# Taking a linear-attention numerator by pairs of token tiles, with the order of a hand-scheduled loop rewritten around it

## The chip, the cores and the metric

The kernel runs on one core of a Trainium2 chip. The metric is the device time of one execution in microseconds (us). Five engines work side by side, each through its own list of instructions in order: TensorE (PE) multiplies, VectorE (DVE), ScalarE (ACT) and GpSimd (POOL) do the elementwise work, SyncE (SP) issues DMAs. An instruction starts when its engine has reached it and the semaphores it waits for have come.

## The reference, cut to what matters

All tensors are fp32; x has 2048 tokens of width 512.

```
h  = x + A(layernorm(x))            # linear attention, 32 heads of 16
h2 = h + B(layernorm(h))            # token-mixing MLP, 2048 -> 1792 -> 2048
A: q, k, v = x @ wqkv, by heads
   phi(t) = [softmax(t @ w_phi), softmax(-t @ w_phi)]      # 32 features a head
   kv  = phi(k)^T v ;  z = sum over tokens of phi(k)
   o   = (phi(q) kv) / (phi(q) z + 1e-6)                    # numerator / denominator
   out = o @ wo
B: u = gelu(h^T w1 + b1) ;  out = (u w2 + b2)^T
```

## The kernel before, in words

The 2048 tokens are 16 tiles of 128 (`NT`). Matmuls that need precision split each operand into a rounded high part and a low rest, and take three products (`mm3`, L60: high·high, high·low, low·high); `split` (L55) makes the parts, the high one on ACT, the low one by a subtraction on another engine.

A first stage (to about 141 us) forms keys, values and the first q tiles, and sums kv and z. Then comes the loop at L630, `for it in range(NT + 3)`, on which the change works. For PE, DVE, ACT and POOL its order is the order in which the code issues (`manual_schedule`, L419); only SP, and everything after the loop, is ordered by the planner. In iteration `it` several token tiles are under way at different steps:

- POOL multiplies the exponentials of q tile it+1 by their weights (`s_pq`, L460) and forms `ez` for tile it+3 (`s_ez`, L442), from which DVE takes the denominator (`s_den`, L451 to L457: a long reduce, then five short steps) and so the weights `w`.
- DVE takes the logits of a later q tile from PSUM (`q_logits`: L151, L152, L145), POOL forms their negative half (`negate`, L159 and L160), ACT the exponentials (`q_exp`, L171), DVE their sums (`q_sums`, L216). `q_mm` projects the next q tile on PE, until all 16 are done in iteration 4.
- `s_tr(it)` (L521): PE transposes the eight 128x128 blocks of the weighted tile into the PSUM tile `tn` (one buffer), and ACT copies them to `pht` in two halves (L527).
- `s_num` (L536): sixteen small fp32 matmuls, 64 rows by 32 columns each, that stream `pht` of one tile (128 columns) against kv into `tn` again; ACT rounds the result to `oh` (L547), DVE takes the rest to `ol` (L552).
- `s_wo` (L554): twelve 128x512 matmuls of `oh` and `ol` with wo into `po` (one PSUM buffer). `s_h` (L564) adds x on DVE, which frees `po`, and sends h out. `s_moments` (ACT, L574 to L576), `s_rstd` (POOL, L579 and L580) and `s_hn` (ACT L584 and L57, POOL L58) normalise h into `hs`, in two parts.
- `fill(p)` (L616): six 128x512 matmuls of `hs` of one token tile with w1, for the pair p of MLP column blocks, accumulated over all 16 tiles into `pu`. The loop takes pairs 0 and 1, one tile behind the other; the other five pairs, and what the loop has not filled, follow after it. `fill_load` (L611) loads two tiles' worth of w1, ACT rounds it (`whi`, L604), and `flush` (L593) has DVE subtract (`wlo`, L596) at a place that the loop chooses.

On PE an iteration runs numerator of tile it-1, wo of tile it-2, transposes of tile it, a q tile, and fills from iteration 4 on (`LAG`, L28). On DVE `s_h` stands fourth in the list, the flush some places behind it. After the loop PE finishes the seven pairs, takes gelu, and multiplies with w2 (L764, from about 383 us).

Of the kernel before, what the change touches and what calls it, by code (L numbers as in the profile page):

```python
# [9 lines left out]
F32 = mybir.dt.float32  # L10
F32R = mybir.dt.float32r
# [13 lines left out]
Q_AT = (4, 6, 8, 9, 11, 13)  # L25
V_NOT = (0, 1, 11)
SUMS = 8
LAG = 4  # L28
WARM = 9
EPS = 1e-5  # L30

# [2 lines left out]
def block_kernel(ctx: ExitStack, tc: tile.TileContext, x, xT, wT, phic, wo, w1, b1, w2, b2,  # L34
# [25 lines left out]
    def mm3(o, ah, al, bh, bl, first, last):  # L60

        nc.tensor.matmul(o, ah, bh, start=first, stop=False)  # L62
        nc.tensor.matmul(o, ah, bl, start=False, stop=False)  # L63
        nc.tensor.matmul(o, al, bh, start=False, stop=last)  # L64
# [90 lines left out]
    def negate():  # L155

        if MN:
            ev, mx, mn = MN.pop(0)
            nc.gpsimd.tensor_sub(mn, mn, mx)  # L159
            nc.gpsimd.tensor_sub(ev[:, :, 1], mn.unsqueeze(3).to_broadcast([P, NPR, 2, DH]), ev[:, :, 0])  # L160

    def turns(*lists):

        return [ops[i] for i in range(max(map(len, lists))) for ops in lists if i < len(ops)]

    def run(*lists):
        for op in turns(*lists):
            op()
# [197 lines left out]
    def q_logits(lag):  # L366
        n = q["logits"]
        if n < min(NT, q["mm"] - lag + NT * (q["mm"] == NT)):
            EQ[n] = big.tile([P, NG, P], F32, name="eq", tag="big")
            q["logits"] += 1  # L370
            return logit_ops(PS[n], EQ[n], n >= len(Q_AT))
        return []
# [7 lines left out]
    def q_sums(lag):  # L380
        n = q["sum"]
        if n < min(NT, q["exp"] - lag + NT * (q["exp"] == NT)):
            q["sum"] += 1
            return q_sum(n)
        return []
# [54 lines left out]
    def s_ez(t):  # L440
        EZ[t] = az.tile([P, NG, P], F32, name="ez")
        nc.gpsimd.tensor_mul(EZ[t], EQ[t], zB)  # L442

    def s_den(t):


        tz = az.tile([P, NPR, 2, 2], F32, name="tz")
        den = az.tile([P, NPR, 2], F32, name="den")
        W[t] = az.tile([P, NPR, 2, 2], F32, name="w", bufs=3)
        other = SQ[t]  # L450
        return [lambda: nc.vector.reduce_sum(tz.rearrange("p g c h -> p (g c h)"), heads(EZ[t]), axis=AX.X),  # L451
                lambda: nc.vector.scalar_tensor_tensor(tz[:, :, 0], other[:, :, 1], 1e-6, tz[:, :, 0],
                                                       op0=ALU.mult, op1=ALU.add),
                lambda: nc.vector.tensor_mul(tz, other, tz),
                lambda: nc.vector.reduce_sum(den, tz.rearrange("p g c h -> p g h c"), axis=AX.X),
                lambda: nc.vector.reciprocal(den, den),
                lambda: nc.vector.tensor_mul(W[t], other, den.unsqueeze(2).to_broadcast([P, NPR, 2, 2]))]  # L457

    def s_pq(t):
        nc.gpsimd.tensor_mul(heads(EQ[t]), heads(EQ[t]), W[t].rearrange("p g c h -> p (g c h)").unsqueeze(2).to_broadcast([P, 2 * H, DH]))  # L460

    def lead(it, mm):

        if 0 <= it + 3 < NT:
            s_ez(it + 3)
        negate()
        for _ in range(mm):
            q_mm()
        q_exp(0)
# [49 lines left out]
    HN, HT, PHT, OS, PO, VE = {}, {}, {}, {}, {}, {}  # L519

    def s_tr(t):  # L521
        PHT[t] = ak.tile([P, NG, P], F32, name="pht")
        ptr = ps_t.tile([P, 2, 4, P], F32, name="tn")
        for g in range(NG):
            nc.tensor.transpose(ptr[:, g // 4, g % 4, :], EQ[t][:, g, :], ident)  # L525
        for half in range(2):
            nc.scalar.activation(PHT[t][:, half * 4:half * 4 + 4, :], ptr[:, half], AF.Copy)  # L527

    def s_kv():

        pt = ps_o.tile([P, 2, P], F32, name="po")
        for b in range(2):
            nc.tensor.transpose(pt[:, b, :], kvS[:, 2 * b:2 * b + 2, :].rearrange("p n f -> p (n f)"), ident)
        nc.scalar.activation(kvB, pt, AF.Copy)

    def s_num(t):  # L536

        pn = ps_t.tile([P, 2, 4, P], F32, name="tn")[:, :, 0:2]
        for b in range(2):
            for c in range(4):  # L540
                for r in range(2):
                    rows, cols = slice(64 * r, 64 * r + 64), slice(32 * c, 32 * c + 32)
                    nc.tensor.matmul(pn[cols, r, b, :], kvB[rows, b, cols], PHT[t][rows, 4 * b + c, :],  # L543
                                     start=True, stop=True, skip_group_check=True)
        oh = ak.tile([P, 2, 2, P], F32R, name="oh")
        ol = ak.tile([P, 2, 2, P], F32R, name="ol")
        nc.scalar.activation(oh, pn, AF.Copy)  # L547
        OS[t] = oh, ol, pn

    def s_ol(t):  # L550
        oh, ol, pn = OS[t]
        return [lambda: nc.vector.tensor_sub(ol, pn, oh)]  # L552

    def s_wo(t):  # L554
        oh, ol, _ = OS.pop(t)
        PO[t] = po = ps_o.tile([P, D], F32, name="po")
        for j in range(4):
            mm3(po, oh[:, j // 2, j % 2, :], ol[:, j // 2, j % 2, :], woh[:, j, :], wol[:, j, :], j == 0, j == 3)

    def s_x(t):  # L560
        HT[t] = ak.tile([P, D], F32, name="h", bufs=4)
        nc.sync.dma_start(HT[t], x[t * P:(t + 1) * P, :])

    def s_h(t):  # L564

        h = HT[t]
        VE[t] = ak.tile([P, 4], F32, name="ve2", bufs=3)
        nc.vector.scalar_tensor_tensor(h, PO.pop(t), 1.0, h, op0=ALU.mult, op1=ALU.add, accum_out=VE[t][:, 2:3])
        nc.sync.dma_start(out[t * P:(t + 1) * P, :], h)

    def s_moments(t):

        junk = ak.tile([P, D], F32, name="hj", bufs=1)
        nc.scalar.activation(VE[t][:, 1:2], VE[t][:, 2:3], AF.Copy, scale=-1.0 / D)  # L574
        nc.scalar.activation(junk, HT[t], AF.Square, bias=VE[t][:, 1:2], accum_out=VE[t][:, 3:4])
        nc.scalar.activation(VE[t][:, 0:1], VE[t][:, 3:4], AF.Identity, scale=(1.0 + EPS) / D, bias=eps2)  # L576
# [5 lines left out]
    def s_hn(t):  # L582
        hn = ak.tile([P, D], F32, name="hn")
        nc.scalar.activation(hn, HT[t], AF.Identity, scale=r2[:, t:t + 1], bias=VE[t][:, 1:2])  # L584
        HN[t] = big.tile([P, 2, D], F32R, name="hs", tag="big")
        split(HN[t][:, 0], HN[t][:, 1], hn, nc.gpsimd)
# [6 lines left out]
    def flush():  # L593
        while LATER:
            wl_, raw, wh_ = LATER.pop(0)
            LO.append(nc.vector.tensor_sub(wl_, raw, wh_).ins)  # L596
# [14 lines left out]
    def fill_load(p):  # L611
        if FL[p] < NT:
            WI[p, FL[p]] = stream(w1v, FL[p], 2, p * 256, 256)
            FL[p] += 2

    def fill(p, pool=None):  # L616

        t = FN[p]
        FN[p] = t + 1
        if FL[p] <= t:  # L620
            fill_load(p)
            flush()
        if t == 0:
            PU[p] = [pool.tile([P, D], F32, name="pu", tag="pu") for _ in range(2)]
        a, b = WI[p, t - t % 2]
        for c in range(2):
            mm3(PU[p][c], a[:, t % 2, c * P:(c + 1) * P], b[:, t % 2, c * P:(c + 1) * P],
                HN[t][:, 0], HN[t][:, 1], t == 0, t == NT - 1)

    for it in range(NT + 3):  # L630
        if 0 <= it < NT:
            s_x(it)
        if 0 <= it - 1 < NT:
            s_num(it - 1)
        if 0 <= it - 3 < NT:
            s_moments(it - 3)
        if 0 <= it - 2 < NT:
            s_wo(it - 2)
        if it == 1:
            run(q_logits(0))  # L640
            q_mm()
        if 0 <= it < NT:
            s_tr(it)
        if it == 0:
            s_kv()
        if 0 <= it + 1 < NT:
            s_pq(it + 1)
        if 0 <= it - 3 < NT:
            s_rstd(it - 3)
        lead(it, 1)  # L650
        den = s_den(it + 2) if it + 2 < NT else []
        ql = q_logits(1)
        ops = turns((s_ol(it - 1) if 0 <= it - 1 < NT else []) + ql + (q_sums(0) if it > 0 else []), den)

        at = 7 if ql else 3
        ops[at:at] = [flush]
        ops[3:3] = [lambda: s_h(it - 2)] if 0 <= it - 2 < NT else []
        run(ops)
        if it > 0:
            negate()  # L660
        if 0 <= it - 3 < NT:
            s_hn(it - 3)
        if FN[0] <= it - LAG:
            fill(0, ps_f)
        for _ in range(2):
            if q["logits"] == NT and FN[1] <= it - LAG:
                fill(1, ps_q)
        for p in range(2):
            if it >= LAG - 2 and FL[p] <= FN[p] + 1:
                fill_load(p)  # L670
    flush()
    ms.close()
# [197 lines left out]
```

## Time and profile before

| what | value |
|---|---|
| median of three runs | 530.43 us (530.4 to 531.09) |
| the profiled execution | 530.48 us |
| its span in the trace | 528.7 us, so 1.8 us lie around it |
| PE busy | 521.3 us, 99% of the span |
| DVE, ACT, POOL busy | 378.8, 272.2, 230.9 us |
| granted TensorE clock | 0.998 |
| the loop's PE work | about 142 to 271 us |

A row of the timeline gives start, duration, engine, source line, operation and `out<-in` with shapes. Durations of neighbours on one engine overlap, since each row includes the end of the pipeline; what an instruction costs its engine is the distance from its start to the start of the next. Each plain fp32 matmul stands in the trace as two records, so the numerator's sixteen appear as x32.

### The profile page before, as it was taken

How to read it: one execution, taken by the hardware profiler on the slowest of the kernel's cores; microseconds unless marked ns; L12 is line 12 of the kernel's file. 1: busy time of each engine (PE TensorE's matmuls, PEld its weight loads, DVE VectorE, ACT ScalarE, POOL GpSimd, SP SyncE). 2: the span in 40 equal slices, each digit the busy share in tenths (PEclk: the TensorE clock that was granted, in tenths of full speed). 3: DMA queues.
4: the chain of work that ended last, by engine and by line, in shares of the span. 5: the costliest groups of instructions: out<-in, count | busy, mean ns of one | idle time of the engine just before them, and what ended most of it. 6: DMA issues, size and time to landing. Idle time of an engine off the chain costs nothing.

```text
span 528.7 us, 9887 instructions
## 1 busy us (share of the span) xinstructions
PE 521.3 (99%) x3872; PEld 450.0 (85%) x3872; DVE 378.8 (72%) x680; ACT 272.2 (51%) x460; POOL 230.9 (44%) x190
## 2 busy tenths in 40 slices
PE   8999999999999999999999999999999999999996
PEld 7888888887877777777888888888899999999996
DVE  6993999876899888773426424835668878987784
ACT  6998833525237776676657323526444243343340
POOL 2589699876999988985335000000001101101110
PEclk9999999999999999999999999999999999999999
DMA  8634300012303223333255333542015466535631
GB/s 315 199 116 119 90 33 21 1 45 97 102 1 100 73 89 119 121 121 120 81 178 161 104 97 98 161 119 81 20 41 113 134 152 151 128 122 121 160 73 48
DMA packets 45487, 55.85 MB, mean 106 GB/s; under 512 B 3968, under 2 KB 33024, under 8 KB 45440
## 3 DMA queue, kind: packets, MB, share of 16 engines
q1 hardware_dynamic: 43136, 51.38, 30.7%
q0 software_dynamic: 2016, 3.67, 5.2%
q8 instruction: 30, 0.49, 0.4%
q10 hardware_dynamic: 288, 0.17, 0.1%
q14 instruction: 17, 0.14, 0.1%
HBM read 46.81 MB, written 8.39 MB: 104 GB/s over the span
## 4 chain that ended last, share of the span: by engine, by line
PE 95%; DVE 3%; DMA 1%; ACT 0%; issue 0%; DVEq 0%
PE py L764 26%; PE pu L62 12%; PE pu L64 12%; PE pu L63 12%; PE po L62 3%; PE pv L63 3%; PE pv L64 3%; PE pv L62 3%; PE po L63 3%; PE po L64 3%; PE tn L525 3%; PE pk_ps L62 2%; PE pk_ps L64 2%; PE pk_ps L63 2%; PE tn L543 2%; PE kvp L207 2%
## 5 line engine op out<-in xcount | busy, mean ns | idle before, releaser
L802 POOL DMA_DIRECT2D out<-ot x14 | 12.5, 1000 | 211.9 <-DVE ot L800 211.9
L764 PE MATMUL py<-uf,whi 128*128 128x256 f32 x560 | 96.2, 283 | 0.0
L57 ACT ACTIVATE whi<-wraw 128x1792 fp32r<-128x1792 f32 x28 | 47.7, 1705 | 77.9 <-PE py L764 70.5
L62 PE MATMUL pu<-hs,whi 128*128 128x512 f32 x224 | 87.4, 393 | 0.0
L63 PE MATMUL pu<-hs,whi 128*128 128x512 f32 x224 | 87.2, 389 | 0.0
L64 PE MATMUL pu<-hs,wlo 128*128 128x512 f32 x224 | 87.0, 390 | 0.2 <-DVE wlo L596 0.2
L764 PEld LDWEIGHTS py<-uf,whi 128*128 128x128 f32 x560 | 83.3, 192 | 0.0
L596 DVE TENSOR_TENSOR wlo<-wraw,whi 128x512 fp32r<-128x512 f32 x56 | 45.1, 816 | 48.5 <-ACT whi L604 48.1
L764 PE MATMUL py<-uf,wlo 128*128 128x256 f32 x280 | 69.9, 283 | 0.0
L58 DVE TENSOR_TENSOR wlo<-wraw,whi 128x1792 fp32r<-128x1792 f32 x28 | 56.6, 2022 | 14.0 <-ACT whi L57 13.9
L604 ACT ACTIVATE whi<-wraw 128x512 fp32r<-128x512 f32 x56 | 34.4, 627 | 45.4 <-PE pu L63 41.4
L64 PEld LDWEIGHTS pu<-hs,wlo 128*128 128x128 f32 x224 | 42.0, 188 | 9.2 <-DVE wlo L596 0.6
L764 PEld LDWEIGHTS py<-uf,wlo 128*128 128x128 f32 x280 | 49.7, 192 | 0.0
L63 PEld LDWEIGHTS pu<-hs,whi 128*128 128x128 f32 x224 | 42.1, 188 | 8.4
L62 PEld LDWEIGHTS pu<-hs,whi 128*128 128x128 f32 x224 | 42.1, 188 | 8.4
L442 POOL TENSOR_TENSOR ez<-eq,zB 128x1024 f32<-128x1024 f32 x16 | 38.8, 2428 | 3.9 <-ACT zB L489 3.9
L764 PE MATMUL py<-un,whi 128*128 128x256 f32 x224 | 38.4, 283 | 0.0
L195 POOL TENSOR_TENSOR pk<-pk,sk 128x1024 f32<-128x1024 f32 x16 | 31.1, 1944 | 9.8 <-DVE sk L194 9.0
L527 ACT ACTIVATE pht<-tn 128x512 f32<-128x512 f32 x32 | 17.4, 596 | 33.4 <-PE tn L525 33.4
L764 PEld LDWEIGHTS py<-un,whi 128*128 128x128 f32 x224 | 33.2, 192 | 0.1
L460 POOL TENSOR_TENSOR eq<-eq,w 128x1024 f32<-128x1024 f32 x16 | 31.0, 1940 | 2.9 <-DVE w L457 2.9
L199 POOL TENSOR_TENSOR zacc<-zacc,pk 128x1024 f32<-128x1024 f32 x13 | 31.4, 2415 | 0.6
(165 smaller groups left out, 1185.3 us busy)
## 6 DMA issues: line engine op xcount, KB each, us to landing
wraw<-in_w SPq DMA_DIRECT2D x112, 256.0 KB, 2.9
xraw<-in_xT SPq DMA_DIRECT2D x16, 256.0 KB, 3.0
xh<-in_x SPq DMA_DIRECT2D x16, 256.0 KB, 2.7
h<-in_x SPq DMA_DIRECT2D x16, 256.0 KB, 3.5
out<-h SPq DMA_DIRECT2D x16, 256.0 KB, 2.0
out<-ot POOLq DMA_DIRECT2D x14, 256.0 KB, 4.6
wraw<-in_wT SPq DMA_DIRECT2D x12, 256.0 KB, 4.8
wo<-in_wo SPq DMA_DIRECT2D x4, 256.0 KB, 4.2
```

Source lines behind the costliest of these rows:

```text
L57: nc.scalar.activation(hi, src, AF.Copy)
L58: lo_engine.tensor_sub(lo, src, hi)
L62: nc.tensor.matmul(o, ah, bh, start=first, stop=False)
L63: nc.tensor.matmul(o, ah, bl, start=False, stop=False)
L64: nc.tensor.matmul(o, al, bh, start=False, stop=last)
L195: nc.gpsimd.tensor_mul(heads(PK[t]), heads(PK[t]), sk.unsqueeze(2).to_broadcast([P, 2 * H, DH]))
L199: nc.gpsimd.tensor_add(zacc, zacc, PK[t])
L442: nc.gpsimd.tensor_mul(EZ[t], EQ[t], zB)
L460: nc.gpsimd.tensor_mul(heads(EQ[t]), heads(EQ[t]), W[t].rearrange("p g c h -> p (g c h)").unsqueeze(2).to_broadcast([P, 2 * H, DH]))
L596: LO.append(nc.vector.tensor_sub(wl_, raw, wh_).ins)
L604: nc.scalar.activation(wh_, raw, AF.Copy)
L764: nc.tensor.matmul(o, a[x], b[:, y], start=start and i == 0, stop=stop and i == 2, skip_group_check=True)
```

## The change

The numerator is taken once for two token tiles, in even iterations: `pht`, `oh`, `ol` hold pairs (one buffer of twice the size in place of two), the sixteen matmuls stream 256 columns, and ACT and DVE take their parts tile by tile. PE's order becomes, in even iterations, numerator of the pair, q tile or fills, wo, transposes; in odd ones q tile or fills, transposes, wo. `fills` takes one tile of pair 1 and then one of pair 0, from iteration 6 and 5 on; before, pair 1 took two in iteration 5. `s_h` and, ahead of it, the flush come last on DVE. The moments stand behind `q_exp` in even iterations and behind the copies of the transposes in odd ones. `s_hn` is issued in even iterations alone, for two tiles.

```diff
-LAG = 4
+LAG = 5
     def s_tr(t):
-        PHT[t] = ak.tile([P, NG, P], F32, name="pht")
+        j, i = divmod(t, 2)
+        if i == 0:
+            PHT[j] = ak.tile([P, NG, 2, P], F32, name="pht", bufs=1)
...
-            nc.scalar.activation(PHT[t][:, half * 4:half * 4 + 4, :], ptr[:, half], AF.Copy)
+            nc.scalar.activation(PHT[j][:, half * 4:half * 4 + 4, i, :], ptr[:, half], AF.Copy)
-    def s_num(t):
-        pn = ps_t.tile([P, 2, 4, P], F32, name="tn")[:, :, 0:2]
+    def s_num(j):
+        pn = ps_t.tile([P, 2, 4, P], F32, name="tn")
...
-                    nc.tensor.matmul(pn[cols, r, b, :], kvB[rows, b, cols], PHT[t][rows, 4 * b + c, :],
+                    nc.tensor.matmul(pn[cols, r, 2 * b:2 * b + 2, :], kvB[rows, b, cols], PHT[j][rows, 4 * b + c, :, :],
...
-        nc.scalar.activation(oh, pn, AF.Copy)
-        OS[t] = oh, ol, pn
+        pv = pn.rearrange("p r (b i) s -> p i r b s", i=2)
+        for i in range(2):
+            nc.scalar.activation(oh[:, i], pv[:, i], AF.Copy)
+        OS[j] = oh, ol, pv
+    def s_ol(j):
+        return [lambda i=i: nc.vector.tensor_sub(ol[:, i], pv[:, i], oh[:, i]) for i in range(2)]
         if FL[p] <= t:
             fill_load(p)
+        if any(part is WI[p, t - t % 2][1] for part, _, _ in LATER):
             flush()
+    def fills(it):
+        if FN[1] < it - LAG:
+            fill(1, ps_q)
+        if FN[0] <= it - LAG:
+            fill(0, ps_f)
     for it in range(NT + 3):
-        if 0 <= it < NT:
-            s_x(it)
-        if 0 <= it - 1 < NT:
-            s_num(it - 1)
-        if 0 <= it - 3 < NT:
-            s_moments(it - 3)
-        if 0 <= it - 2 < NT:
-            s_wo(it - 2)
+        even = it % 2 == 0
+        if 0 <= it + 1 < NT:
+            s_pq(it + 1)
+        if it == 0:
+            s_tr(0)
+            s_kv()
         if it == 1:
             run(q_logits(0))
             q_mm()
-        if 0 <= it < NT:
-            s_tr(it)
-        if it == 0:
-            s_kv()
-        if 0 <= it + 1 < NT:
-            s_pq(it + 1)
-        if 0 <= it - 3 < NT:
+            s_tr(1)
+        if it > 1 and even:
+            if it <= NT:
+                s_num(it // 2 - 1)
+            if it >= 4:
+                s_hn(it - 4)
+        den = s_den(it + 2) if it + 2 < NT else []
+        if it > 1 and even and it <= NT:
+            ol = s_ol(it // 2 - 1)
+            run(ol[:1] + den[:1] + ol[1:])
+            den = den[1:]
+        if it < NT:
+            s_x(it)
+        if it < 3 and it + 3 < NT:
+            s_ez(it + 3)
+        negate()
+        q_mm()
+        fills(it)
+        q_exp(0)
+        logits = q_logits(1)
+        if it >= 3 and even:
+            s_moments(it - 3)
+        if it > 1 and even and it - 2 < NT:
+            s_wo(it - 2)
+        if 1 < it < NT:
+            s_tr(it)
+        if it > 1 and not even and it - 2 < NT:
+            s_wo(it - 2)
+        if it >= 3 and not even:
+            s_moments(it - 3)
+        if it >= 3:
             s_rstd(it - 3)
-        lead(it, 1)
-        den = s_den(it + 2) if it + 2 < NT else []
-        ql = q_logits(1)
-        ops = turns((s_ol(it - 1) if 0 <= it - 1 < NT else []) + ql + (q_sums(0) if it > 0 else []), den)
-
-        at = 7 if ql else 3
-        ops[at:at] = [flush]
-        ops[3:3] = [lambda: s_h(it - 2)] if 0 <= it - 2 < NT else []
-        run(ops)
+            if it + 3 < NT:
+                s_ez(it + 3)
+        run(logits + (q_sums(0) if it > 0 else []), den)
+        flush()
+        if 0 <= it - 2 < NT:
+            s_h(it - 2)
         if it > 0:
             negate()
-        if 0 <= it - 3 < NT:
+        if it >= 3 and even:
             s_hn(it - 3)
-        if FN[0] <= it - LAG:
-            fill(0, ps_f)
-        for _ in range(2):
-            if q["logits"] == NT and FN[1] <= it - LAG:
-                fill(1, ps_q)
         for p in range(2):
-            if it >= LAG - 2 and FL[p] <= FN[p] + 1:
+            if it >= LAG - 3 + p and FL[p] <= FN[p] + 2 * (FN[p] > 0):
                 fill_load(p)
```

More of the change, by code (lines that the diff above doesn't have):

```diff
@@ L542, in s_num @@
                     rows, cols = slice(64 * r, 64 * r + 64), slice(32 * c, 32 * c + 32)
-                    nc.tensor.matmul(pn[cols, r, b, :], kvB[rows, b, cols], PHT[t][rows, 4 * b + c, :],
+                    nc.tensor.matmul(pn[cols, r, 2 * b:2 * b + 2, :], kvB[rows, b, cols], PHT[j][rows, 4 * b + c, :, :],
                                      start=True, stop=True, skip_group_check=True)
-        oh = ak.tile([P, 2, 2, P], F32R, name="oh")
-        ol = ak.tile([P, 2, 2, P], F32R, name="ol")
-        nc.scalar.activation(oh, pn, AF.Copy)
-        OS[t] = oh, ol, pn
-    def s_ol(t):
-        oh, ol, pn = OS[t]
-        return [lambda: nc.vector.tensor_sub(ol, pn, oh)]
+        oh = ak.tile([P, 2, 2, 2, P], F32R, name="oh", bufs=1)
+        ol = ak.tile([P, 2, 2, 2, P], F32R, name="ol", bufs=1)
+        pv = pn.rearrange("p r (b i) s -> p i r b s", i=2)
[3 more added lines that the diff above has]
+    def s_ol(j):
+        oh, ol, pv = OS[j]
+        return [lambda i=i: nc.vector.tensor_sub(ol[:, i], pv[:, i], oh[:, i]) for i in range(2)]
     def s_wo(t):
-        oh, ol, _ = OS.pop(t)
+        oh, ol, _ = OS[t // 2]
+        i = t % 2
         PO[t] = po = ps_o.tile([P, D], F32, name="po")
         for j in range(4):
-            mm3(po, oh[:, j // 2, j % 2, :], ol[:, j // 2, j % 2, :], woh[:, j, :], wol[:, j, :], j == 0, j == 3)
+            mm3(po, oh[:, i, j // 2, j % 2, :], ol[:, i, j // 2, j % 2, :], woh[:, j, :], wol[:, j, :], j == 0, j == 3)
     def s_x(t):
```

## The prediction

> **What bounds the kernel now.** I read the page first: its busy times, then the chain that ended last.
>
> ```profile
> PE 521.3 (99%) x3872; PEld 450.0 (85%) x3872; DVE 378.8 (72%) x680; ACT 272.2 (51%) x460; POOL 230.9 (44%) x190
> ...
> PE 95%; DVE 3%; DMA 1%; ACT 0%; issue 0%; DVEq 0%
> ```
>
> PE is busy for 99% of the span, and 95% of the chain is PE. Then the list of waits of PE from 141 to 276 us, the loop, with PE's rows of one iteration.
>
> ```profile
> PE pu L64 <- DVE wlo L596: 0.2, 1, 0.2
> ```
>
> One wait, 0.2 us, in the whole loop. So time can be won here only by taking work off PE (and 0.2), and every wait that the change brings is paid in full.
>
> ```profile
> 153.11 0.39 PE L64 MATMUL pu<-wqh,xs 128*128 128x512 f32 x1
> 153.43 0.67 PE L543 MATMUL tn<-pht,kvB 64*32 64x128 f32 x32
> 154.03 0.50 PE L62 MATMUL po<-woh,oh 128*128 128x512 f32 x1
> 154.36 0.40 PE L63 MATMUL po<-wol,oh 128*128 128x512 f32 x1
> ...
> 156.65 0.39 PE L64 MATMUL po<-woh,ol 128*128 128x512 f32 x1
> 156.88 1.03 PE L525 MATMUL tn<-ident,eq 128*128 128x128 f32 x8
> 157.67 0.48 PE L62 MATMUL pu<-wqh,xs 128*128 128x512 f32 x1
> ```
>
> Start to start, a 128x512 matmul costs (156.65-154.36)/10 = 0.23, so a fill of six is 1.37 and a wo or q tile of twelve 2.73. The numerator runs 154.03-153.43 = 0.60; around it the steps are 0.32 and 0.33 in place of 0.23, so it costs 0.60+0.09+0.10 = 0.79 a tile. Transposes cost 0.79 and some 0.09 behind them.
>
> **The change on PE.** The chain, earlier, has a plain fp32 matmul of 512 columns:
>
> ```profile
> 127.43 1.72 PE pk_ps L488 x4
> ```
>
> Four records in 1.72, 0.43 each, so 128 columns stream for 0.107. The numerator's 32 records, each on one of eight 64x32 parts of the array, make four rounds of 0.107, 0.43 of its 0.60; the other 0.17 is starting and ending. With 256 columns I take 0.60+0.43 = 1.03 for a pair, with the edges 1.22, against 2 x 0.79 = 1.58: **0.36 a pair, 2.9 us for eight pairs**. Bounds: 0.60 if something other than streaming sets it (then 6.3), 1.20 if nothing is shared (then 1.5). Nothing else leaves PE: three fills (15+15 before, 14+13 after) move behind the loop, 4.1 us, where they cost the same; they are missing in iterations 4 and 5.
>
> **The change on the other engines: the same instructions in another order.** In before the order holds PE's inputs ready; the question is where they come late. Three things set it.
>
> *First, POOL's wait in iteration 3.* POOL still has h's scale ahead of `ez`, as before, so in that point the change doesn't alter what its title says. But the moments it waits for now stand on ACT behind the copies of the odd iteration's transposes.
>
> ```profile
> 161.85 0.19 ACT L574 ACTIVATE ve<-ve 128x1 f32<-128x1 f32 x1
> ...
> 162.93 0.29 ACT L576 ACTIVATE ve<-ve,eps 128x1 f32<-128x1 f32 x1
> ...
> 165.11 1.09 ACT L527 ACTIVATE pht<-tn 128x512 f32<-128x512 f32 x2 [1.89 <-PE tn L525]
> ```
>
> ```profile
> 163.30 0.55 POOL L579 TENSOR_TENSOR r<-ve,mhalf 128x1 f32<-128x1 f32 x1
> ```
>
> Moments take 163.22-161.85 = 1.4, copies 1.0 from 1.07 after the transposes start. Going forward from 146.2, where PE's order first differs (q tile, transposes, q tile, numerator, q tile, wo, transposes, q tile), transposes 3 start at 163.0, so the moments end at 166.5 and the scale starts at 166.5 instead of 163.30. POOL has ended its `s_pq` at 163.3: it idles 3.2 us, and `ez` of tile 6, the negation, `s_pq` and the next scale, queued behind, all slip. Denominator 6 waits for `ez` on DVE, and DVE's second `ol`, the logits, the flush and `s_h` wait behind it.
>
> *Second, DVE and POOL now leave the same `ez` together.* In iteration 4, POOL goes from the end of one `ez` to the next over negation, `hs`, `s_pq`, scale; in before the same list, in another order, is
>
> ```profile
> 172.60 2.41 POOL L442 TENSOR_TENSOR ez<-eq,zB 128x1024 f32<-128x1024 f32 x1
> 174.97 0.26 POOL L159 TENSOR_TENSOR mn<-mn,mx 128x32 f32<-128x32 f32 x1
> ...
> 176.32 1.28 POOL L58 TENSOR_TENSOR hs<-hn,hs 128x512 fp32r<-128x512 f32 x1
> 177.57 1.93 POOL L460 TENSOR_TENSOR eq<-eq,w 128x1024 f32<-128x1024 f32 x1
> 179.47 0.54 POOL L579 TENSOR_TENSOR r<-ve,mhalf 128x1 f32<-128x1 f32 x1
> ...
> 180.23 2.40 POOL L442 TENSOR_TENSOR ez<-eq,zB 128x1024 f32<-128x1024 f32 x1
> ```
>
> 180.23-174.97 = 5.26. DVE meanwhile goes from the denominator's reduce to the flush over `ol`, three logit steps, two sums and five short steps. In before an equal list, with `s_h` for `ol` (0.61 both), is
>
> ```profile
> 170.01 1.21 DVE L451 TENSOR_REDUCE tz<-ez 128x64 f32<-128x1024 f32 x1
> ...
> 175.42 0.23 DVE L457 TENSOR_TENSOR w<-smq,den 128x64 f32<-128x64 f32 x1
> ```
>
> 5.41 and 0.14 for the last step, 5.55. So the flush reaches DVE 0.3 after POOL has started `ez`.
>
> *Third, what that costs.*
>
> ```profile
> 188.30 2.39 POOL L442 TENSOR_TENSOR ez<-eq,zB 128x1024 f32<-128x1024 f32 x1
> ```
>
> ```profile
> 188.49 0.68 DVE L568 SCALAR_TENSOR_TENSOR h<-po,h 128x512 f32<-128x512 f32 x1
> 189.10 0.09 DVE L568 DVE_READ_ACCUMULATOR h<-po,h 128x1 f32 x1
> 189.10 2.14 DVE L596 TENSOR_TENSOR wlo<-wraw,whi 128x512 fp32r<-128x512 f32 x1
> ...
> 239.68 1.29 DVE L596 TENSOR_TENSOR wlo<-wraw,whi 128x512 fp32r<-128x512 f32 x2
> ```
>
> Two `wlo` with POOL idle take 1.29, 0.65 each; the one that begins 0.8 into an `ez` ends 0.55 after that `ez` (191.24 against 190.69): it is held for all of it. In before `s_h` stood ahead of the flush; now it stands behind, and `po` is free only after `s_h`.
>
> [...]
>
> So, iteration 4 and 5: scale 166.5, `ez` 167.7 to 170.2 (0.4 added where a `wlo` is in its way), DVE's reduce 170.2, flush 175.8; POOL's next `ez` 175.5 to 177.9; `wlo` ends 178.4, `s_h` of tile 2 at 179.0. PE: transposes 4 at 173.4, one fill (with 0.25 of waiting for `hs`, whose low part comes at 174.7), transposes 5 to 176.85, then wo of tile 3, which wants `po`: **2.3 us of waiting**. In before three more fills stood in these two iterations. Were the flush first, `s_h` would end at 177.2 and the wait be 0.4, but then the second `ol` of iteration 6, behind the `ez` that ends near 186, would hold the transposes for 1.1: the lateness stays with POOL, which has no gap until iteration 7.
>
> From iteration 6 fills give PE 6.9 us an iteration. Writing on in the same way, I find the third matmul of fill (1, tile 2) waiting 0.45 for its `wlo` in iteration 8, wo of tile 7 waiting 0.65 for `s_h` behind a held `wlo` in iteration 9, and 0.25 in iteration 10: 0 to 1.35. Each hangs on a few tenths; I take half, 0.7. From iteration 12 the sums have ended, and I find none.
>
> *Covers.* Copies of transposes (2.1 after their start): under wo, or fills; if gone, up to 0.7. `oh` and `ol`:
>
> ```profile
> 154.20 0.60 ACT L547 ACTIVATE oh<-tn 128x512 fp32r<-128x512 f32 x1 [0.42 <-PE tn L543]
> ```
>
> ```profile
> 154.83 0.69 DVE L552 TENSOR_TENSOR ol<-tn,oh 128x512 fp32r<-128x512 f32 x1 [0.64 <-ACT oh L547]
> ```
>
> 0.77 after the numerator's start (1.2 with 256 columns) and 0.63 on: first `ol` done 2.5 us after the start, the reduce and the second `ol` by 4.3, where wo wants the first at 4.2 and the transposes `tn` at 6.5. SP's queue:
>
> ```profile
> wraw<-in_w SPq DMA_DIRECT2D x112, 256.0 KB, 2.9
> ...
> h<-in_x SPq DMA_DIRECT2D x16, 256.0 KB, 3.5
> ```
>
> Loads and stores are as many as before; x lands 3.5 after its issue and is wanted two iterations (13.9) later, w1 2.9 after, an iteration ahead of its `whi`. I cost them at nothing; a load held past that would be paid in full.
>
> At the end h of tile 15 is normalised while PE fills:
>
> ```profile
> 266.02 0.69 DVE L568 SCALAR_TENSOR_TENSOR h<-po,h 128x512 f32<-128x512 f32 x1 [1.56 <-POOL ve L580]
> ```
>
> ```profile
> 271.46 1.29 POOL L58 TENSOR_TENSOR hs<-hn,hs 128x512 fp32r<-128x512 f32 x1 [1.59 <-ACT hs L57]
> ```
>
> 6.7 from sum to `hs`, and PE shows no wait, as the planner puts other pairs' fills in. With two iterations' fills fewer there is still as much to put in; if it keeps the written order, 4.1 of cover leaves some 2.5. I take 0.
>
> **Sum**, against the profiled 530.48 (the median is 0.05 lower): -2.9 -0.2 +0.25 +2.3 +0.7 = +0.15, so **530.6 us**.
>
> **The rivals.** (a) *PE is not held*: POOL's gap of 3.2 is real, but if the flush comes ahead of `ez` each time, only the 0.25 and the 0.4 stay: 530.48-3.1+0.65 = 528.0. For it: DVE and POOL miss each other by 0.3 us. Against: the late `ez` holds `ol` anyway. (b) *The ring closes, and it is slower*: transposes of an odd iteration, copies, moments, scale, `ez`, `hs` and `s_pq`, `ez`, `wlo`, `s_h`, wo. By the rows 1.1+1.0+1.4+0.8+2.4+3.9+2.4+0.6+0.7 = 14.3 from transposes to `po` free, and the wo that needs it stands a pair of iterations and 0.9 later, 13.9+0.9 = 14.8 us. The slack is 0.5 us; it decides from 0.5 us of further delay in the ring (a `wlo` ahead of the scale is 0.65). With 0.5 lost in each of six pairs on top of the forecast: 533.6. (c) *The numerator saves least*: with 1.20 a pair, 1.4 less, 532.0.
>
> [...]
>
> **How the numbers follow.** Forecast 0.40, held within 529.4 to 531.6; (a) 0.30; (b) 0.25; (c) 0.05. A measurement of this kernel tells about 0.2%, 1.06 us, from no change. Faster: (a) but for a little; slower: (b), (c); so 0.31, 0.40, 0.29. The range runs from (a), 527.8, to near (b), 533.0: its own 0.40 with most of (a) and (b) inside.
>
> **What would show it.** PE's row of the numerator: starts 1.0 apart from the next, once a pair. POOL idle some 3 us before its first scale, released by ACT. One PE wait of 2 us for `h` near 177 us; a `wlo` of 2 to 3 us ahead of it. If PE waits nowhere, (a); if for `h` in every odd iteration, (b). A PE pace other than 0.23, or a wait behind 271 us, would make all this wrong.

## The result, and the profile after

| | before | after |
|---|---|---|
| median of 10 runs | 530.88 us (530.4 to 531.19) | 532.14 us (531.79 to 534.85) |
| ratio | | 1.003, 95% interval 1.0018 to 1.0043 |
| the profiled execution | 530.48 us | 532.60 us |
| its span | 528.7 us | 530.8 us |

The change makes the kernel 0.3% slower, by 1.26 us. The forecast was 530.6 us; the time lies inside the range, 527.8 to 533.0.

The page of after: busy times, and the shares of the chain that ended last.

```profile
PE 521.8 (98%) x3616; PEld 450.3 (85%) x3616; DVE 381.9 (72%) x680; ACT 272.1 (51%) x460; POOL 231.0 (44%) x190
...
PE 89%; DVE 7%; ACT 2%; POOL 1%; issue 0%; DVEq 0%; POOLq 0%
```

PE issues 256 records fewer, as the title says, and yet is busy 0.5 us longer. The chain now runs over DVE for 7% of the span, in place of 3%: somewhere PE waits for it. The list of waits of PE in the loop, 141 to 276 us, says where:

```profile
PE po L62 <- DVE h L574: 2.3, 2, 2.0
```

Two waits for `h`; before had one, of 0.2 us, for a `wlo`. First the gain. PE's rows around one numerator:

```profile
226.25 0.39 PE L64 MATMUL po<-woh,ol 128*128 128x512 f32 x1
226.56 1.09 PE L546 MATMUL tn<-pht,kvB 64*32 64x256 f32 x32
227.59 0.50 PE L62 MATMUL pu<-hs,whi 128*128 128x512 f32 x1
227.92 0.40 PE L63 MATMUL pu<-hs,whi 128*128 128x512 f32 x1
```

Start to start it takes 227.59-226.56 = 1.03 for a pair, with steps of 0.31 and 0.33 at its edges: 1.22, as worked out ahead of the run. Eight pairs save 2.88 us.

Now the loss. POOL, where its lateness begins, and at the next `ez`:

```profile
167.22 0.55 POOL L585 TENSOR_TENSOR r<-ve,mhalf 128x1 f32<-128x1 f32 x1 [3.04 <-ACT ve L582]
...
168.39 2.40 POOL L442 TENSOR_TENSOR ez<-eq,zB 128x1024 f32<-128x1024 f32 x1
...
176.01 2.37 POOL L442 TENSOR_TENSOR ez<-eq,zB 128x1024 f32<-128x1024 f32 x1
```

DVE at that next `ez`:

```profile
176.37 2.56 DVE L602 TENSOR_TENSOR wlo<-wraw,whi 128x512 fp32r<-128x512 f32 x1
178.85 0.68 DVE L574 SCALAR_TENSOR_TENSOR h<-po,h 128x512 f32<-128x512 f32 x1
```

POOL idles 3.04 us for the moments; the flush arrives 0.36 us after POOL has started the second `ez`, and its `wlo`, 0.65 us by itself, takes 2.56 us: it ends 0.55 us after that `ez`. The sum of h stands behind it. PE, which has sent the transposes at 176.59, wants `po`:

```profile
176.59 1.03 PE L527 MATMUL tn<-ident,eq 128*128 128x128 f32 x8
179.60 0.50 PE L62 MATMUL po<-woh,oh 128*128 128x512 f32 x1 [1.97 <-DVE h L574]
179.93 0.39 PE L63 MATMUL po<-wol,oh 128*128 128x512 f32 x1
...
181.09 0.63 PE L62 MATMUL po<-woh,oh 128*128 128x512 f32 x1
181.52 0.63 PE L63 MATMUL po<-wol,oh 128*128 128x512 f32 x1
...
183.23 0.63 PE L64 MATMUL po<-woh,ol 128*128 128x512 f32 x1
183.78 1.40 PE L546 MATMUL tn<-pht,kvB 64*32 64x256 f32 x32
185.11 0.50 PE L62 MATMUL pu<-hs,whi 128*128 128x512 f32 x1
```

Without the wait, wo would have started 0.88 after the transposes, so it costs 179.60-176.59-0.88 = 2.13 us. Then look at the durations: from 181.09 on a 128x512 matmul takes 0.63 in place of 0.39, and its successor comes 0.43 later in place of 0.23. The table by stretches (PE busy first, the granted TensorE clock third from the end) names the cause:

```profile
174.00:177.00 3.00, 2.96 (x19) 2.36 (x18) 2.97 (x8) 1.87 (x4) 2.92 (x5) 1.00 0.00 0
177.00:180.00 3.00, 1.03 (x8) 0.75 (x7) 3.00 (x4) 2.97 (x6) 2.92 (x3) 1.00 0.35 89
180.00:182.00 2.00, 2.00 (x9) 1.58 (x8) 2.00 (x5) 1.44 (x4) 2.00 (x3) 0.77 0.83 252
182.00:184.00 2.00, 2.00 (x13) 1.15 (x19) 1.97 (x5) 0.00 (x0) 1.92 (x3) 0.50 0.05 16
184.00:186.00 2.00, 2.00 (x36) 1.12 (x23) 1.32 (x5) 0.69 (x2) 2.00 (x2) 0.88 0.01 4
```

The granted clock (1.00 is full speed) falls to 0.50 after the wait and comes back near 184.5 us. PE counts as fully busy all that time, so neither the busy share nor the list of waits shows this loss. By starts: the last six matmuls of wo take 183.78-181.09 = 2.69 in place of 6 x 0.23 + 0.09 = 1.46, and the numerator 185.11-183.78 = 1.33 in place of 1.03; 1.5 us together.

So, against before, in the profiled executions: -2.88 (numerator) -0.37 (before's `wlo` wait, by starts: from the distances between PE's starts, which also hold the slower step behind a wait, 0.33 in place of 0.23 at 179.60 in after) +0.32 (the first fill waits for `hs`) +2.13 (`po`) +0.44 (wo of tile 7 waits for `h`, near 209 us) +1.53 (half clock) = +1.17. From the last sum of kv to the first matmul of the second MLP layer the traces give 382.72-142.10 = 240.62 in before and 384.74-143.00 = 241.74 in after: +1.12. (The other 0.9 of the two spans' difference lies in the first stage, which the change doesn't touch; it started the loop at 142.1 to 143.1 in the profiles of this case.)

### The profile page after: what moved, and what is told of

It reads as the page before. It is cut to its first block, busy times and chain, and to the rows that moved or that the text cites. A ratio compares the mean times of both kernels' runs of the same rounds, so it can differ in the third digit from the quotient of the medians.

```text
span 530.8 us, 9386 instructions
## 1 busy us (share of the span) xinstructions
PE 521.8 (98%) x3616; PEld 450.3 (85%) x3616; DVE 381.9 (72%) x680; ACT 272.1 (51%) x460; POOL 231.0 (44%) x190
## 4 chain that ended last, share of the span: by engine, by line
PE 89%; DVE 7%; ACT 2%; POOL 1%; issue 0%; DVEq 0%; POOLq 0%
PE py L791 26%; PE pu L62 12%; PE pu L63 11%; PE pu L64 11%; PE pv L63 3%; PE pv L64 3%; PE pv L62 3%; PE pk_ps L62 2%; PE pk_ps L64 2%; PE pk_ps L63 2%; PE po L62 2%; PE po L64 2%; PE po L63 2%; PE kvp L207 2%; PE tn L527 2%; PE pu L268 1%
## 5 line engine op out<-in xcount | busy, mean ns | idle before, releaser
L602 DVE TENSOR_TENSOR wlo<-wraw,whi 128x512 fp32r<-128x512 f32 x56 | 47.2, 846 | 53.1 <-ACT whi L610 50.1
```

## The experiments

The theory after the result: **(A)** POOL's late `ez` puts `ez` and `wlo` side by side, the `wlo` ahead of the sum of h holds `po`, and the idle time then costs PE a half clock on top. Rivals: **(B)** only the order of flush and sum on DVE matters, not POOL; **(C)** the half clock is no consequence of the wait; **(D)** the numerator's gain is less than it looks, or has another source. The expectations name their theories for themselves: their Theory A is (B) here, and their Theory B is the first half of (A).

**The sum ahead of the flush, in every iteration (e1_sum_before_flush).**

```diff
-        flush()
         if 0 <= it - 2 < NT:
             s_h(it - 2)
+        flush()
```

> Theory A (one wait: the flush, put ahead of s_h on DVE, is held by POOL's ez, so po comes free 2 us late, and the 2 us of idle PE bring the half clock): with s_h ahead of the flush the 2.0 us wait near 177 us is gone, no stretch has a granted clock of 0.5, and the time falls by 1.9 to 2.5 us against the changed kernel, to about 530 us. Theory B (the root is POOL's ez, 2 to 3 us late since iteration 3, whose scale waits for moments behind the copies; the order on DVE only picks where PE pays): the wait comes back as waits for q logits and for the second ol in iteration 6, some 1.5 us together, and the time falls by less than 1 us.

Measured: 532.10 us (before 531.05), ratio 1.0024 (1.0008 to 1.004). PE's waits in the loop:

```profile
PE pu L64 <- DVE wlo L602: 1.7, 2, 1.0
PE tn L527 <- DVE ol L557: 0.6, 1, 0.6
```

The wait for `h` is gone, and no clock of 0.5 is left in the loop. In its place two fills wait for `wlo`, 1.04 and 1.14 by starts, and the transposes of iteration 6 some 0.76 for the second `ol`. On DVE that `ol` stands behind a reduce that waits for POOL's late `ez`:

```profile
186.69 1.22 DVE L451 TENSOR_REDUCE tz<-ez 128x64 f32<-128x1024 f32 x1 [1.25 <-POOL ez L442]
187.82 0.68 DVE L557 TENSOR_TENSOR ol<-tn,oh 128x512 fp32r<-128x512 f32 x1
```

(B) falls: swapping the order only chooses what is late. The prediction had this wait too, in what it wrote against a flush in time: 1.1 us for that `ol`.

**The moments ahead of the copies (e2_moments_early)**, so that POOL isn't late to begin with.

```diff
+        if it >= 3 and not even:
+            s_moments(it - 3)
         if 1 < it < NT:
             s_tr(it)
         if it > 1 and not even and it - 2 < NT:
             s_wo(it - 2)
-        if it >= 3 and not even:
-            s_moments(it - 3)
```

> Moments ahead of the transposes' copies in odd iterations, the flush still ahead of s_h. POOL's scale of tile 0 then starts near 165.3 us in place of 167.2. Theory A: the flush still starts inside an ez and is held, so PE's wait near 177 us stays about 2 us and the time within 0.5 us of the changed kernel. Theory B: everything behind that scale comes 1.9 us or more earlier, the wait falls to 0.4 us or less, no half clock, and the time falls by 2 to 3 us, to about 529.5 us.

Measured: 529.79 us (before 531.05), 0.9975 (0.9966 to 0.9985). POOL's first scale, and PE's waits:

```profile
164.59 0.55 POOL L585 TENSOR_TENSOR r<-ve,mhalf 128x1 f32<-128x1 f32 x1 [1.02 <-ACT ve L582]
```

```profile
PE tn L546 <- ACT pht L529: 1.0, 1, 1.0
PE po L62 <- DVE h L574: 0.5, 1, 0.5
```

POOL idles 1.02 in place of 3.04, and its first scale comes 2.63 us earlier (2.0 when counted from the last sum of kv, which came 0.64 earlier in this trace). The wait for `h` shrinks from 2.0 to 0.5, and the time falls by 2.35 us: the moments' place on ACT is the root of the loss in this order. A new wait of 1.0 for the copies is what (A) did not have: in the other odd iterations the copies now stand behind the moments.

**Both at once (e3_both).** The two edits above together.

> Both edits: s_h ahead of the flush, moments ahead of the copies. By either theory no wait of PE over 0.5 us in the loop and no half clock; what is left is the numerator's 2.9 us and the 0.2 us that the kernel before waits: about 3 us under the kernel before, 528 us. If it is still over 529.5, the gain of the numerator is smaller than its rows say, or waits of a third kind are there.

Measured: 533.43 us (before 531.05), 1.0042 (1.003 to 1.0054), slower than either alone. PE's waits, then the stretches around the longer one:

```profile
PE pu L64 <- DVE wlo L602: 2.2, 2, 2.0
PE tn L546 <- ACT pht L529: 1.9, 2, 1.1
```

```profile
197.00:200.00 3.00, 1.00 (x11) 0.53 (x4) 3.00 (x2) 2.73 (x6) 3.00 (x2) 1.00 0.56 178
200.00:202.00 2.00, 2.00 (x7) 1.58 (x7) 2.00 (x4) 0.89 (x3) 2.00 (x2) 0.67 0.45 138
202.00:204.00 2.00, 2.00 (x6) 1.54 (x6) 1.86 (x6) 0.00 (x0) 1.92 (x4) 0.50 0.34 128
```

My expectation was wrong: two repairs don't add. On DVE the flush of iteration 7, two `wlo` behind the sum, now runs from 196.27 to 199.72, 3.45 us in place of 1.29, beside an `ez` from 196.34 that itself takes 2.83 in place of 2.40; the fill that wants the second waits 2.17.

```profile
196.27 3.45 DVE L602 TENSOR_TENSOR wlo<-wraw,whi 128x512 fp32r<-128x512 f32 x2
```

```profile
196.34 2.83 POOL L442 TENSOR_TENSOR ez<-eq,zB 128x1024 f32<-128x1024 f32 x1
```

What repeats is the tail: another tile, another buffer, some 2 us of waiting, and again the clock at 0.50 behind it.

**Each edit only where the trace asks for it (e4_two_places)**: the moments early in iteration 3 alone, the sum ahead of the flush in iteration 4 alone.

```diff
+        if it == 3:
+            s_moments(it - 3)
         if 1 < it < NT:
             s_tr(it)
...
-        if it >= 3 and not even:
+        if it > 3 and not even:
...
-        flush()
+        if it != 4:
+            flush()
         if 0 <= it - 2 < NT:
             s_h(it - 2)
+        if it == 4:
+            flush()
```

> Moments ahead of the copies in iteration 3 alone, s_h ahead of the flush in iteration 4 alone; the rest as changed. Theory B (late ez of iteration 3 is the root): with POOL early from iteration 3 on and po free in time, none of the later waits has a cause; PE waits less than 0.5 us in all in the loop, and the time is the kernel before less 2.9 and 0.2, about 3 us under it (528 us). Rival: each iteration's order is tight for itself, so that later iterations (7 to 10) show waits of 1 us or more for copies, wlo or h as in the two runs before: 529 us or more.

Measured: 529.41 us (before 531.01), 0.9969 (0.9958 to 0.9981). What is left of PE's waits:

```profile
PE pu L64 <- DVE wlo L602: 0.6, 2, 0.4
```

No wait for `h`, no half clock. By starts the waits are 0.46 and 0.56, and some 0.2 near 206 us: 1.2 of the 1.4 us that are missing to the 3 us expected. The rest is open. The numerator's gain is real, which speaks against (D).

**The pair as two halves (e5_halves):** e4_two_places with 32 matmuls of 128 columns in place of 16 of 256.

```diff
-        for b in range(2):
-            for c in range(4):
...
-                    nc.tensor.matmul(pn[cols, r, 2 * b:2 * b + 2, :], kvB[rows, b, cols], PHT[j][rows, 4 * b + c, :, :],
+        for i in range(2):
+            for b in range(2):
+                for c in range(4):
...
+                        nc.tensor.matmul(pn[cols, r, 2 * b + i, :], kvB[rows, b, cols], PHT[j][rows, 4 * b + c, i, :],
```

> As e4, but the pair's numerator in 32 matmuls of 128 columns in place of 16 of 256. If its time is rounds of streaming plus one start and end (8 rounds of 0.11 us either way), a pair still takes about 1.03 us and the time stays within 0.4 us of e4: the gain is that two tiles share edges and start. If each matmul has a fixed cost that 256 columns spread, a pair takes 1.2 us or more and the time is 1.4 us or more over e4.

Measured: 529.76 us (before 531.01), 0.9979 (0.997 to 0.9988). PE around one pair:

```profile
223.02 1.16 PE L547 MATMUL tn<-pht,kvB 64*32 64x128 f32 x64
224.11 0.50 PE L62 MATMUL pu<-hs,whi 128*128 128x512 f32 x1
```

A pair takes 224.11-223.02 = 1.09, against 1.03 with wide matmuls and 2 x 0.60 in before. Of the 0.36 a pair, 0.06 comes from the width; 0.11 from starting and ending once, and 0.19 from one pair of edges fewer. The saving is as large as predicted, and most of it comes, as the prediction worked it out, from putting two bursts side by side; only the 0.06 needs the wide matmuls.

**A wait of chosen length, elsewhere (e6_wait_short, e7_wait_long):** e4_two_places with reduces on DVE ahead of the sum in iteration 12, whose results nobody uses: eight of them in the first (shown), ten in the second.

```diff
+        if it == 12:
+            dj = ak.tile([P, 16], F32, name="dj", bufs=1)
+            for k in range(8):
+                nc.vector.tensor_reduce(dj[:, k:k + 1], PO[it - 2], axis=AX.X, op=ALU.max)
```

> As e4, with eight extra reduces of po on DVE ahead of s_h in iteration 12 (0.6 us each, output unused), so that PE waits some 1.2 us for po ahead of wo in iteration 13, at a place where nothing else is late. If only idle time is paid: 1.2 us over e4. If the granted clock falls after it: a window of 3.4 us at 0.5 and up to 1.7 us more. I expect the idle time alone, as waits of 1.2 us left the clock at 1.0 before.

> As e6 with ten reduces: PE waits some 2.4 us. Theory: a wait over 2 us brings, in most executions, a window of 3.4 us at clock 0.5, which costs about 1.7 us on top: 2.4 to 4.1 us over e4, in two groups. Rival (the half clock near 181 us had another cause): 2.4 us over e4, clock 1.0 throughout.

Measured: 530.90 us (before 531.01; 1.0001, 0.9991 to 1.001) and 532.29 us (1.0029, 1.0016 to 1.0041). PE's row behind the wait, in the first and in the second:

```profile
235.89 0.50 PE L62 MATMUL po<-woh,oh 128*128 128x512 f32 x1 [1.09 <-DVE h L574]
```

```profile
237.20 0.50 PE L62 MATMUL po<-woh,oh 128*128 128x512 f32 x1 [2.28 <-DVE h L574]
```

Against the 0.88 that transposes take, PE lost 1.25 us in the one, which lengthened the kernel by 1.5 against e4_two_places, and 2.45 in the other, which lengthened it by 2.9 (1.39 and 2.54 between the two points named above). Both waits were paid in full, as the prediction said. But in the second the clock stayed at 1.00 behind a wait longer than that of after; of its five executions one, of 533.31 us, has a mean clock of 0.996, the others 0.998 and 0.999. So a wait of over 2 us doesn't always bring the half clock; something besides its length decides, and these runs don't show what (the last section has what the traces measured).

**Loads two ahead, from the start (e8_loads_ahead):** e4_two_places with w1 loaded one step earlier, against its `wlo` waits.

```diff
-            if it >= LAG - 3 + p and FL[p] <= FN[p] + 2 * (FN[p] > 0):
+            if it >= LAG - 3 + p and FL[p] <= FN[p] + 2:
```

> As e4, with the second pair of w1 tiles of both column pairs loaded two or three iterations earlier, so that their wlo are taken in iterations 4 and 5 and not right ahead of the fills. If the two waits of PE for wlo that e4 has left (0.46 and 0.56 us) come from loads that are asked for too late, they go and the time falls by about 1.0 us under e4, to 528.4. Rival: DVE has no room in iterations 4 and 5, the added wlo hold h or ol there, and the time stays within 0.4 us of e4 or rises.

Measured: 531.92 us (before 531.0), 1.0014 (1.0005 to 1.0023). DVE in iteration 5:

```profile
182.45 2.40 DVE L602 TENSOR_TENSOR wlo<-wraw,whi 128x512 fp32r<-128x512 f32 x1 [0.22 <-DMA wraw<-in_w]
184.78 0.68 DVE L574 SCALAR_TENSOR_TENSOR h<-po,h 128x512 f32<-128x512 f32 x1
```

The waits for `wlo` are gone, and the `wlo` that moved into iteration 5 has met an `ez` there, ahead of the sum: PE waits 2.3 us for `h`, and again the clock falls to 0.50, from 185.55 us. Its executions fall into two groups: three of 530.3 to 530.7 us at a clock of 0.998, nine of 531.7 to 532.6 at 0.994 to 0.997, with medians 1.6 us apart. So the half clock is worth about as much as the 1.5 read by starts, and is not there each time.

**The late `ez` in the kernel before (e9_before_late):** before, with the moments of iteration 3 behind its transposes' copies.

```diff
-        if 0 <= it - 3 < NT:
+        if 0 <= it - 3 < NT and it != 3:
             s_moments(it - 3)
...
             s_tr(it)
+        if it == 3:
+            s_moments(it - 3)
```

> The kernel before, with the moments of iteration 3 alone moved behind the copies of its transposes, where the change has them: POOL's scale of tile 0 comes about 4 us later, near 167.6 us, and idles before it. Theory B': the late ez costs PE only because the change has also taken three fills (4.1 us) out of iterations 4 and 5 and put s_h last; in the order of before the slack takes it up: PE waits 0.5 us or less, time within 0.6 us of the kernel before. Rival: the late ez alone is enough, PE waits 2 us or more, over 532.5.

Measured: 531.51 us (530.56 to 532.27, before 531.0), 1.0008 (0.9999 to 1.0017). POOL's first scale:

```profile
168.00 0.55 POOL L579 TENSOR_TENSOR r<-ve,mhalf 128x1 f32<-128x1 f32 x1 [4.42 <-ACT ve L576]
```

POOL idles 4.42 us, more than in after, and PE's list of waits in the loop is empty; between the two points named above it takes 240.63, as before did (240.62). So in this trace the late `ez` does no harm by itself; in after it did together with what else the change does there: the sum behind the flush, and three fills fewer in iterations 4 and 5 (which of the two weighs more, this run doesn't tell). The spread of its ten runs, with clocks near 1.0, I can't explain.

**e8_loads_ahead, with the sum ahead of the flush in iteration 5 too (e10_loads_and_sum):**

```diff
-        if it != 4:
+        if it not in (4, 5):
             flush()
...
-        if it == 4:
+        if it in (4, 5):
             flush()
```

> e8_loads_ahead moved one wlo of w1 into iteration 5, where it was held by an ez ahead of the sum of h, and PE waited 2.3 us for po. This kernel puts the sum ahead of the flush in iteration 5 as well as 4. If the order of those two instructions was the whole cause, the wait for po goes, the wlo waits of e4_two_places stay away, and the time is 528.4 us, 1.0 below e4_two_places (529.4). Rival: the wlo is then held by the same ez and is itself late for its fill, or it delays the next ol behind it; then a PE wait of 0.5 us or more on wlo or ol stands in iteration 6 to 7, and the time is 529.4 us or more.

Measured: 529.29 us (before 530.97), 0.9971 (0.9961 to 0.998). DVE in iterations 5 and 6, and PE's waits:

```profile
183.88 1.76 DVE L602 TENSOR_TENSOR wlo<-wraw,whi 128x512 fp32r<-128x512 f32 x1
185.57 0.68 DVE L557 TENSOR_TENSOR ol<-tn,oh 128x512 fp32r<-128x512 f32 x1
```

```profile
PE po L64 <- DVE ol L557: 1.5, 1, 1.5
PE po L62 <- DVE h L574: 0.2, 1, 0.2
```

The rival is right: `h` is in time, the same `wlo` still stands in the same `ez`, and now the `ol` behind it is late by 1.5 us for wo of tile 4. The time is that of e4_two_places, the best seen here, within what can be told apart.

**PE kept busy through the wait (e11_kept_busy):** after, with nine more matmuls in the gap.

```diff
+        if it == 5:
+            a, b = WI[0, 0]
+            for c in (0, 1, 0):
+                mm3(PU[0][c], a[:, 0, c * P:(c + 1) * P], b[:, 0, c * P:(c + 1) * P],
+                    HN[0][:, 0], HN[0][:, 1], False, False)
         if it > 1 and not even and it - 2 < NT:
             s_wo(it - 2)
```

> The kernel after, with nine more 128x512 matmuls (2.05 us at full clock) on PE ahead of wo of token tile 3 in iteration 5, where PE otherwise waits about 2.1 us for h; they add token tile 0 to pair 0's sums a second and third time, which changes the result. They fill the idle time and cost nothing of it. Theory: the matmuls at half clock behind that wait are caused by the idle time and cost 1.5 us in the profiled execution of after. Then the wait for h falls under 0.3 us, no clock of 0.5 stands near 182 us in any execution, and the time is 531.0 us, or 530.9 to 531.2 (in the profiled execution of after 532.6 - 1.55). Rival: executions of after at a clock of 0.998 to 1.0 took 531.8, so what is not lost to the clock is lost to other waits later in the same ring; then the time is 531.8 and PE shows a new wait of 0.5 us or more between 185 and 215 us.

Measured: 531.21 us (530.85 to 531.56, before 531.13), 0.9998 (0.9987 to 1.0009). PE's waits, and the stretches in which after lost its clock:

```profile
PE pu L64 <- DVE wlo L602: 0.4, 1, 0.4
```

```profile
177.00:180.00 3.00, 3.00 (x17) 2.32 (x15) 3.00 (x4) 2.95 (x6) 2.92 (x3) 1.00 0.38 97
180.00:182.00 2.00, 2.00 (x11) 1.63 (x10) 2.00 (x5) 1.38 (x4) 2.00 (x3) 1.00 0.79 247
182.00:184.00 2.00, 2.00 (x37) 1.07 (x36) 1.97 (x6) 0.32 (x1) 1.92 (x4) 1.00 0.03 9
```

PE does 2 us more work than in after and ends sooner: ratio 0.9998 against 1.003, with intervals that don't meet. The clock is 1.00 in these stretches, and 0.997 to 0.999 on average in all twelve executions. (C) falls: the idle time brought the half clock. Half a microsecond comes back as a later wait for `wlo` (0.53 by starts, at 198 us), as the rival said; its 531.8 isn't reached, and 531.21 stands at the upper end of what the theory gave, 530.9 to 531.2. A lost clock isn't the change's alone: of the 17 executions of before measured beside this run, two, of 533.25 and 533.32 us, have a mean clock of 0.996. No trace shows what held PE there.

## Why the prediction was right and wrong

| step | predicted | measured in the profiled execution |
|---|---|---|
| numerator, a pair | 1.22 (1.03 and edges), -2.9 in all | 1.22, -2.88 |
| the `wlo` wait of before | -0.2 | -0.37 by starts |
| POOL's first scale, idle ahead of it | 166.5, 3.2 us | 167.22, 3.04 us |
| flush behind the start of `ez` | 0.3 us | 0.36 us |
| first fill waits for `hs` | +0.25 | +0.32 |
| wo of tile 3 waits for `po` | +2.3 | +2.13 |
| later waits | +0.7 | +0.44 |
| the clock behind the wait | none | +1.5 |

The mechanism was right: the late scale, the `wlo` held beside `ez`, the sum behind it and the wait for `po`, each where it was placed, and the waits sized within 0.3 us each. Of the three later waits that the 0.7 halved, the trace has only that of wo of tile 7. **The step that failed is the price of the wait: the sum took it as idle time and nothing more, with every matmul at 0.23 us.** The prediction named "a PE pace other than 0.23" among what would make it wrong, and gave it neither a price nor a share. That term, with three small errors (-0.17, +0.07, -0.17) and the later waits' -0.26, turned +0.15 into +1.17, and "within 0.2%", the likeliest class at 0.40, into slower by 0.3%. That the range still holds the time is due to its width, which was drawn for the rivals: in this the prediction was lucky. The slower side, 0.29, was to come by way of a closing ring or a poor numerator; neither happened. The slack that rival (b) found was there: PE waits for `h` twice, not in each pair.

The half clock isn't in every execution. Of the ten of after, seven have a mean clock of 0.991 to 0.995 and took 532.0 us or more; three have 0.998 to 1.0 and took 531.8. Less the 1.53, the seven's median of 532.5 would be 531.0, near the 531.2 of e11_kept_busy; those three lost 0.8 us more than that. No profile of such an execution exists here, so where they lost it stays open; that a later wait takes its place, as in e1_sum_before_flush and e11_kept_busy, is only argued.

Rival (a)'s price, 528.0, was 2.45 us under before, with 0.65 us of waits left. e4_two_places comes to 1.6 us under its before, with the 1.2 us of waits that its trace still shows.

## What to carry to other kernels

Where PE is the bound, a wait is to be priced as its length plus what the clock may do behind it (in after 2.13 us and 1.5 more); after any change look at the granted clock by stretches, since PE at half clock counted as fully busy here (2.00 of the 2.00 us from 182 to 184 in after) and no list of waits named it. When a wait comes from two engines that run a closed ring without a gap, reordering one of them moves it (h, `wlo`, `ol` in turn here); look for the first instruction in the ring that waits for something outside it, here the scale behind the moments, and move that. The small tiled matmuls here gained mostly from being issued in one burst: 0.30 of 0.36 us a pair (e5_halves).

## What the hardware showed

The clock. In after the half clock (0.50 granted) lasts from 181.06 to 184.47 us, 3.41 us, and begins 1.5 us after PE had work again; in e3_both from 200.66 to 204.08, 3.42 us, 0.9 us after; in e8_loads_ahead from 185.55 to 188.96, 3.41 us, beginning while PE still waits. PE had lost 2.13, 2.17 and 2.32 us. A wait of 1.25 us (e6_wait_short) brought none; one of 2.45 us (e7_wait_long) none in its profile.

Here are the 3.41 us ahead of the half clock and the half clock in after, then the stretches of e7_wait_long that share its wait (PE busy first, the granted clock third from the end):

```profile
177.65:181.06 3.41, 1.46 (x6) 1.24 (x7) 3.41 (x5) 3.35 (x8) 3.33 (x4) 1.00 0.54 130
181.06:184.47 3.41, 3.41 (x23) 2.09 (x29) 3.34 (x10) 0.41 (x1) 3.33 (x5) 0.50 0.29 106
```

```profile
233.00:236.00 3.00, 1.92 (x13) 1.47 (x11) 3.00 (x6) 2.33 (x5) 2.59 (x3) 1.00 0.36 93
236.00:239.00 3.00, 1.80 (x8) 1.50 (x9) 2.90 (x7) 1.79 (x6) 1.40 (x2) 1.00 0.23 87
```

PE is idle for 3.41-1.46 = 1.95 us of the 3.41 ahead of the fall in after, for 2.00 in e3_both and 2.10 in e8_loads_ahead. That doesn't tell these from e7_wait_long: there PE is idle for 2.28 us up to 237.20, and the clock stays at 1.00 from 233 to 239 us. So of the four profiled waits over 2 us three brought the half clock and the longest did not; what decides, and why only some executions of one kernel lose the clock, the runs don't show.

A `wlo` that started inside POOL's `ez` ended some 0.55 us behind the end of that `ez`: it took 2.56 us in after (to 178.93, the `ez` to 178.38) and 2.40 in e8_loads_ahead (to 184.85 and 184.31), in place of 0.65. That was in before's rows. New is that POOL can lose too: the `ez` of e3_both that began 0.07 us behind a `wlo` took 2.83 us in place of 2.40.
